# Unread products on TensorE through the head of the run, and two scalar loads moved behind the head of the queues, in a windowed-attention kernel with a gated feed-forward part

## The chip, the cores and the metric

The kernel runs on one core of a Trainium2 chip. The metric is the device time of one execution, in microseconds (us). TensorE is called PE, its weight load PEld, VectorE DVE, ScalarE ACT, GpSimd POOL, SyncE SP.

## What is computed

Two parts, one behind the other; the second takes the output of the first, with the heads side by side, as its x.

```
# q, k, v: 4 batches, 8 heads, 768 positions, 64 wide; n_sink = 4, window = 128
scores = q @ k.T / 8
keep   = (key position < n_sink) or (0 <= query - key < window)
a      = softmax(where(keep, scores, -1e9))          # a / (sum + 1e-9)
x      = a @ v                                        # (4, 768, 512)
h      = relu(x @ w_in);  u, v = halves of h          # w_in (512, 1024)
v_n    = (v - mean) / sqrt(var + 1e-6)                # over 512 columns
v_s    = w_spatial @ v_n + b_spatial                  # w_spatial (768, 768)
out    = (u * v_s) @ w_out                            # w_out (512, 512)
```

w_in and w_out are given in float64; the kernel gets their words and puts the float32 values together itself ("decoding"). n_sink and window are int64 scalars. The kernel has a fast path for 4 and 128 and a general path for anything else; the scalars decide at run time which result stands.

## The kernel before, in words

The work is cut into 48 half tiles: 4 batches, 6 tiles of 128 query positions each, 2 halves of 4 heads. For a half tile PE makes the scores (`sc`), DVE adds the mask and takes the row's smallest value (line 892, `pexp`, `nm`), ACT takes the exponential (line 897), the weights are transposed (in batch 0 by PE, `tr`, line 925, with a copy back to `pT`; later by DMA), PE multiplies them with v (`av`, lines 1005 and 1013), and DVE divides by the sums (`divide`, lines 1020 to 1024, tile `x`). `x` is split into two f16 parts and transposed by DMA (line 1041, `xT`). From `xT` come the v half (`ps_v`, 12 products of 128x512) and, per pair of tiles, the u half (`ps_u`). With a whole batch's v half and w_spatial PE makes `ps_s`, and at the end `ps_o`. Nearly all products are made of three f16 or rounded f32 products (`three`, line 608: high by high, high by low, low by high); in batch 0 the scores and the weights-times-v products are plain f32.

The order of all this is written by a planner in the kernel, class `Plan`. Each piece is added with a rank, its engine, its cost in us, a function that issues it, and the tiles that it reads and writes (`plan.add`). `Plan.order` takes the pieces whose inputs are done, starts the one that can start first in its own account of time (at equal times the one of lower rank), and keeps a ring of buffers per kind of tile. In PSUM there are four banks for `sc` and `tr` together, one double one for `av`, and two for `ps_v`, `ps_u`, `ps_s`, `ps_o` and the one-column products that carry a maximum across partitions (`ps_row`, `ps_col`): that ring is called `mm`. All pieces are then issued in the order of their planned starts, engine by engine, and the engines work their queues off in that order.

The head of the run: SP loads K and q of the first tile, four blocks of w_in's second half, v, and so on (`FIRST_LOADS`). ACT and DVE decode w_in (lines 661 to 671, tile `w`), POOL adds a part (line 674), `all_max` and `scalar` find a scale, and lines 576 and 597 write the two f16 parts (`win`). PE has nothing to do before the first scores.

`read_scalars` (line 35) loads n_sink by SP and window by ACT, each spread over 128 partitions into `words`, as the first DMA of either queue, ahead of the fast path. `tile_kernel` compares them with 4 and 128 after the fast path (lines 1210 to 1216), but the instructions wait only for `words`, and in the built program the conversion (line 41), four comparisons (line 1211), a maximum (line 1213) and a conversion (line 1215) stand at the front of DVE's row. SP reads the flag (line 1216) between two loads of w_in; the other engines read it at the end.

Of the kernel before, what the change touches and what calls it, by code (L numbers as in the profile page):

```python
# [6 lines left out]
F32 = mybir.dt.float32  # L7
# [27 lines left out]
def read_scalars(tc, pool, n_sink, window):  # L35
    nc = tc.nc
    words = pool.tile([P, 4], I32, name="words")
    nc.sync.dma_start(words[:, 0:2], n_sink.bitcast(I32).partition_broadcast(P))
    nc.scalar.dma_start(words[:, 2:4], window.bitcast(I32).partition_broadcast(P))
    wf = pool.tile([P, 4], F32, name="wf")  # L40
    nc.vector.tensor_copy(wf, words)
    return words, wf
# [223 lines left out]
IN_TURN = ("u", "vn", "qkraw", "qp", "pexp", "pT", "p16", "xT", "x16", "av", "sc", "vraw", "vslot0", "vslot1", "vslot2", "vslot3")  # L266
LATENCY = {"PE": 0.25, "d": 0.15, "a": 0.18, "p": 0.12}
# [11 lines left out]
QUEUED = 3.0  # L279
class Plan:  # L280
# [6 lines left out]
    def __init__(self, rings, ring_of):  # L287
        self.pieces, self.rings, self.ring_of = [], rings, ring_of

# [4 lines left out]
    def order(self):  # L294
# [58 lines left out]
        while open_:  # L353
# [46 lines left out]
            for j in after[i]:  # L400
                missing[j] -= 1
                ready[j] = max(ready[j], end)
                if not missing[j]:
                    open_.append(j)
            out.append((t, len(out), f, e))
        if len(out) != n:
            raise RuntimeError("plan: pieces left")
        self.end = max(until.values())
        return [(f, e) for _, _, f, e in sorted(out, key=lambda x: x[:2])]
# [6 lines left out]
def begin(nc, pool):  # L416
# [5 lines left out]
    nc.scalar.activation(first, first, AF.Exp)  # L422
    st.wsp = pool.tile([P, (NT + 1) * S], F32, name="wsp")
# [38 lines left out]
def fast_path(tc, st, qk, v, v0, vs, w_in, w_sp, b_sp, w_out, out):  # L462
# [7 lines left out]
    with (  # L470
# [47 lines left out]
        def next_p16(name):  # L518
# [24 lines left out]
            "ps_o": ("mm", bank("mm")), "ps_row": ("mm", bank("mm")), "ps_col": ("mm", bank("mm")),  # L543
# [617 lines left out]

        W = WHEN
        for t in (0, 2, 4, 5):
            load_v(t)
# [22 lines left out]
        for b in range(B):  # L1187
            gap = W["s gap"]
            for c0 in range(S // TC):
                s0 = 2 * NT * (b + 1) + W["s"] + c0 * (KC * gap + W["s rest"])  # L1190
                for d in range(KC):
                    s_piece(b, c0, d, s0 + d * gap)
                o0 = s0 + KC * gap + W["o"]
                for k in range(TC // P):
                    o_piece(b, c0, k, o0 + k * W["o gap"])
        order = plan.order()
# [5 lines left out]
def tile_kernel(tc, qk, v, v0, vs, n_sink, window, w_in, w_sp, b_sp, w_out, out):  # L1202
    nc = tc.nc
    with tc.tile_pool(name="top", bufs=1) as top:
        with tc.tile_pool(name="first", bufs=1) as pool:
            st = begin(nc, pool)
            words, wf = read_scalars(tc, top, n_sink, window)
            fast_path(tc, st, qk, v, v0, vs, w_in, w_sp, b_sp, w_out, out)
        bad = top.tile([P, 4], F32, name="bad")
        for i, x in enumerate((FAST_N, 0, FAST_W, 0)):  # L1210
            nc.vector.tensor_scalar(bad[:, i:i + 1], wf[:, i:i + 1], float(x), None, op0=ALU.not_equal)
        flag = top.tile([P, 1], F32, name="flag")
        nc.vector.tensor_reduce(out=flag, in_=bad, axis=AX.X, op=ALU.max)
        flagi = top.tile([P, 1], I32, name="flagi")
        nc.vector.tensor_copy(flagi, flag)
        rv = nc.values_load(flagi[0:1, 0:1], min_val=0, max_val=1)
        with tc.If(rv > 0):
            general_path(tc, wf, qk, v, w_in, w_sp, b_sp, w_out, out)
# [45 lines left out]
```

## Time and profile before

| | us |
|---|---|
| median of 3 runs | 443.92 |
| lowest, highest | 441.65, 444.85 |
| span of the profiled execution, first to last instruction | 439.1 |
| what lies around the span, if that execution took the median | 4.8 |
| PE busy | 414.1 |
| DVE busy | 319.1 |
| ACT busy | 272.0 |
| POOL busy | 156.6 |

The profile is of one execution. Times in it count from the span's first instruction. A wait is put down to what ended it last. A stretch is named by its start and end. A transposing load or a scalar load has two times: how long its queue took to issue it, and how long from issue to landing.

### The profile page before, as it was taken

The page shows a single profiled execution, that of the slowest core. Times are in us where ns is not written, and L with a number is a line of the kernel's source. Part 1 is how long each engine was busy: PE and PEld are TensorE (multiplying, and loading weights), DVE is VectorE, ACT ScalarE, POOL GpSimd, SP SyncE. Part 2 cuts the span into 40 slices and gives each one's busy share as a digit, 9 for nine tenths or more (in the row PEclk, how much of TensorE's full clock was granted, in tenths as well). Part 3 has the DMA queues.
Part 4 walks back from the last instruction along what each step waited for, and adds up shares of the span by engine and source line. Part 5 has one row for each costly group of instructions (what it writes and reads, how often), then busy time and mean ns, then how long its engine had stood idle before and what let it go on. Part 6 is the DMA issues. An engine that isn't in the chain of part 4 may idle for free.

```text
span 439.1 us, 9802 instructions
## 1 busy us (share of the span) xinstructions
PE 414.1 (94%) x3669; PEld 323.9 (74%) x3669; DVE 319.1 (73%) x937; ACT 272.0 (62%) x584; POOL 156.6 (36%) x214
## 2 busy tenths in 40 slices
PE   2689999999989999999999999999999999999994
PEld 1467777777677877877778878868778778688882
DVE  3999988689999885878986966788994645143430
ACT  3898978789977565469864754677664353232211
POOL 4426565645735432238351512343541112000000
PEclk9999999999999999999999999999999999999998
DMA  5999414549976784279964673567723822200011
GB/s 215 384 344 296 119 29 115 169 118 196 175 132 162 182 173 133 41 209 208 189 170 123 134 154 87 73 187 154 135 69 98 137 61 64 73 2 24 25 48 57
DMA packets 117928, 59.98 MB, mean 137 GB/s; under 512 B 100240, under 2 KB 103920, under 8 KB 117872
## 3 DMA queue, kind: packets, MB, share of 16 engines
q1 hardware_dynamic: 117728, 59.27, 55.3%
q8 instruction: 31, 0.51, 0.5%
q14 instruction: 25, 0.20, 0.1%
q10 hardware_dynamic: 144, 0.00, 0.0%
HBM read 28.58 MB, written 6.29 MB: 79 GB/s over the span
## 4 chain that ended last, share of the span: by engine, by line
PE 85%; DVE 9%; DMA 2%; issue 1%; ACT 1%; POOL 0%; SPq 0%; ACTq 0%; DVEq 0%
PE ps_s L608 21%; PE ps_o L608 16%; PE ps_v L608 13%; PE ps_u L608 12%; PE sc L887 6%; PE av L1013 4%; PE sc L881 3%; DVE pexp L892 2%; PE tr L925 2%; PE av L997 1%; PE av L999 1%; PE av L998 1%; DMA qkraw<-qk_t 1%; PE av L1005 1%; DVE wsp L597 1%
## 5 line engine op out<-in xcount | busy, mean ns | idle before, releaser
L608 PE MATMUL ps_s<-wsp,vn 128*128 128x256 f16 x864 | 101.0, 273 | 1.6 <-DVE wsp L597 0.8
L608 PEld LDWEIGHTS <-vn 128*128 128x128 f16 x864 | 82.5, 98 | 14.8 <-issue 2.7
L897 ACT ACTIVATE pexp<-pexp,nm 128x260 f32<-128x260 f32 (+1 forms) x192 | 81.2, 484 | 6.2 <-DVE nm L892 6.0
L608 PE MATMUL ps_o<-wout,g 128*128 128x512 f32 x288 | 70.2, 399 | 0.0
L608 PE MATMUL ps_u<-xT,win 128*128 128x256 f16 x576 | 69.0, 273 | 0.4 <-ACT u L1110 0.4
L608 PE MATMUL ps_v<-win,xT 128*128 128x512 f16 x288 | 66.2, 379 | 1.1 <-ACT u L1110 1.1
L608 PEld LDWEIGHTS ps_o<-wout,g 128*128 128x128 f32 x288 | 53.1, 188 | 12.8
L608 PEld LDWEIGHTS <-win 128*128 128x128 f16 x576 | 54.9, 98 | 10.0 <-issue 1.7
L1131 DVE SCALAR_TENSOR_TENSOR g<-ps_s,isc,b_bc 128x256 f32<-128x256 f32 x48 | 23.1, 481 | 39.6 <-PE ps_s L608 38.2
L608 PEld LDWEIGHTS <-xT 128*128 128x128 f16 x288 | 27.0, 98 | 31.5 <-issue 2.2
L574 ACT CAST g<-g 128x256 fp32r<-128x256 f32 x39 | 15.8, 404 | 50.5 <-DVE g L1135 48.3
L590 DVE TENSOR_TENSOR p<-pexp,p 128x1024 f16<-128x1024 f32 (+2 forms) x56 | 40.6, 747 | 8.6 <-ACT p L574 8.6
L590 POOL TENSOR_TENSOR x<-x,x 128x512 f16<-128x512 f32 x24 | 31.2, 1299 | 22.5 <-ACT x L574 21.4
L887 PE MATMUL sc<-kring,qp 64*128 64x260 f32 (+1 forms) x432 | 35.3, 296 | 0.0
L1110 ACT ACTIVATE u<-ps_u,icu 128x256 f32<-128x256 f32 x48 | 22.3, 469 | 17.2 <-PE ps_u L608 17.2
L887 PEld LDWEIGHTS sc<-kring,qp 64*128 64x128 f32 x432 | 28.1, 186 | 6.3 <-issue 4.2
L1078 POOL TENSOR_TENSOR rs<-rs,mhalf 128x1 f32<-128x1 f32 x24 | 16.2, 676 | 46.0 <-DVE rs L1072 42.5
L1157 ACT COPY ob<-ps_o 128x512 f32<-128x512 f32 x24 | 14.1, 586 | 27.9 <-PE ps_o L608 27.9
L574 ACT CAST p<-pexp 128x32 f16<-128x32 f32 (+2 forms) x52 | 30.7, 620 | 0.5
L1068 DVE BATCH_NORM_STATS2 st<-vr 128x6 f32<-128x512 f32 x24 | 16.5, 689 | 17.2 <-ACT vr L1062 17.2
L590 DVE TENSOR_TENSOR g<-g,g 128x256 fp32r<-128x256 f32 x41 | 22.5, 550 | 8.5 <-ACT g L574 7.9
L997 PE MATMUL av<-vring,pT 128*128 128x65 f16 x264 | 27.7, 193 | 0.0
(143 smaller groups left out, 762.5 us busy)
## 6 DMA issues: line engine op xcount, KB each, us to landing
qkraw<-qk_t SPq DMA_DIRECT2D x18, 512.0 KB, 4.4
out<-ob SPq DMA_DIRECT2D x24, 256.0 KB, 2.3
vraw<-v_s SPq DMA_DIRECT2D x18, 256.0 KB, 4.4
dec<-w_in SPq DMA_DIRECT2D x8, 512.0 KB, 6.9
wsp<-w_sp_t SPq DMA_DIRECT2D x6, 384.0 KB, 6.1
dec<-w_out SPq DMA_DIRECT2D x4, 512.0 KB, 4.5
wsp<-qk_t SPq DMA_DIRECT2D x6, 256.0 KB, 5.5
qkraw<-qk_t SPq DMA_DIRECT2D x6, 256.0 KB, 4.4
```

Source lines behind the costliest of these rows:

```text
L574: nc.scalar.copy(o, x)
L590: eng[e].tensor_tensor(out=o, in0=x, in1=hi, op=ALU.subtract)
L608: nc.tensor.matmul(o, a, m, start=(i == 0), stop=(i == n - 1))
L887: nc.tensor.matmul(o, qp[rows, qi, hp, :], keys(kring[:, ki], rows), start=(m == 0), stop=(m == 2))
L897: nc.scalar.activation(po, po, AF.Exp, bias=nm()[:, h2 + q:h2 + q + 1], scale=-1.0)
L997: nc.tensor.matmul(o[:, h], ph, vh, start=(t < 2 and j == 0), stop=False)
L1013: nc.tensor.matmul(o[:, h], pT[:, q * P:(q + 1) * P], v_whole(kt)[:, g:g + D + 1], start=(t < 2 and j == 0), stop=(j == nb - 1 and (t < 2 ...
L1068: nc.vector.bn_stats(s6, vr())
L1078: nc.gpsimd.tensor_tensor(out=vals["rs", i], in0=vals["rs", i], in1=mhalf, op=ALU.pow)
L1110: plan.add(r + WHEN["u relu"], "a", 0.36, lambda e: nc.scalar.activation(tl("u", (b, c0))[:, d, :], tl("ps_u", i)[:, :TC], AF.Relu, scale= ...
L1131: nc.vector.scalar_tensor_tensor(out=g(), in0=tl("ps_s", i)[:, :TC], scalar=vals["s", "sp"][1], in1=b_bc[:, t0:t0 + TC], op0=ALU.mult, op1 ...
L1157: plan.add(r + WHEN["o copy"], "a", 0.5, lambda e: nc.scalar.copy(tl("ob", i), tl("ps_o", i)), [("ps_o", i)], [("ob", i)])
```

## The change

The scalars' loads and comparisons become a class with two steps, `load` and `compare`. Both loads go through SP. The two steps are added to the plan as pieces of rank 27 (`SCALARS_AT`), one on SP, one on DVE; the rank is far behind those of the first tiles (a half tile's rank is its number, from 0 to 47), so that the planner puts them where nothing of lower rank can start.

POOL writes a tile `warm` (128x512, bf16) as its first own work, by an iota. PE gets products of `warm` with itself, 128x128 by 128x256, into a tile of the ring `mm` that nobody reads: 24 as the piece of the lowest rank (-300), and one as a piece of rank 3.2, which reads `x` of the second tile and so waits for its division; the bank is held until then. When the order is made, the planner looks at PE's planned gaps up to that last piece; into each gap of over 0.6 us it puts products for six tenths of the gap less 0.2 us, at 0.11 us each: 82 in twelve gaps, 18 of them between the 24 and the first real product.

```
+    def load(self):
+        for i, x in enumerate(self.sources):
+            self.nc.sync.dma_start(self.words[:, 2 * i:2 * i + 2], x.bitcast(I32).partition_broadcast(P))
+
+    def compare(self):
+        v = self.nc.vector
+        v.tensor_copy(self.wf, self.words)
+        for i, x in enumerate((FAST_N, 0, FAST_W, 0)):
+            v.tensor_scalar(self.bad[:, i:i + 1], self.wf[:, i:i + 1], float(x), None, op0=ALU.not_equal)
+        v.tensor_reduce(out=self.flag, in_=self.bad, axis=AX.X, op=ALU.max)
+        v.tensor_copy(self.flagi, self.flag)
...
+WARM_N, WARM_FIRST = 256, 24
+SCALARS_AT = 27.0
...
         self.end = max(until.values())
+        pe = sorted(x for x in out if x[3] == "PE")
+        last = next(k for k, x in enumerate(pe) if x[1] == self.warm_until)
+        for k in range(last):
+            gap = pe[k + 1][0] - self.ends[pe[k][1]]
+            if gap > 0.6:
+                out.append((self.ends[pe[k][1]], pe[k][1] + 0.5, self.between(0.6 * gap - 0.2), "PE"))
...
+    st.warm = pool.tile([P, 512], BF16, name="warm")
+    nc.gpsimd.iota(st.warm, pattern=[[1, 512]], base=1, channel_multiplier=3, allow_small_or_imprecise_dtypes=True)
...
-            "ps_o": ("mm", bank("mm")), "ps_row": ("mm", bank("mm")), "ps_col": ("mm", bank("mm")),
+            "ps_o": ("mm", bank("mm")), "warm": ("mm", bank("mm")), "ps_row": ("mm", bank("mm")), "ps_col": ("mm", bank("mm")),
...
+        def keep_warm(n):
+            for _ in range(n):
+                nc.tensor.matmul(tl("warm", 0)[:, :WARM_N], st.warm[:, :P], st.warm[:, :WARM_N], start=True, stop=True)
+
         W = WHEN
+        plan.add(-300, "PE", 0.1, lambda e: keep_warm(WARM_FIRST), [], [("warm", 0)])
+        plan.between = lambda t: (lambda e: keep_warm(int(t * 1000 / 110)))
+        plan.add(SCALARS_AT, "SP", 0.8, lambda e: scalars.load(), [], [("words", 0)], dma=0.3)
+        plan.add(SCALARS_AT, "d", 1.3, lambda e: scalars.compare(), [("words", 0)], [("flag", 0)])
...
+        plan.add(3.2, "PE", 0.1, lambda e: keep_warm(1), [("x", (0, 1))], [("warm", 0)])
         order = plan.order()
```

Line numbers of the changed kernel are some 30 higher than those of before for the same work.

PE's row from the start: `sc` are the first tile's scores, `tr` the transposes of the weights, `av` the weights times v, `ps_row` the first of the products that carry a maximum. Before:

```order
L1260 UNCONDITIONAL_BRANCH
L881 MATMUL sc<-wsp,qkraw 128x128 x8
L925 MATMUL tr<-ident,pexp 128x128 x4
L1013 MATMUL av<-vring,pT 128x65 x4
L628 MATMUL ps_row<-ident,allmax_m 1x128
```

After, with the repeated pairs of a weight load and a product left out (42, 4, 13, 5 and 2 of them):

```order
L1291 UNCONDITIONAL_BRANCH
L1193 LDWEIGHTS warm
L1193 MATMUL warm<-warm 128x256
...
L910 MATMUL sc<-wsp,qkraw 128x128 x4
...
L954 MATMUL tr<-ident,pexp 128x128 x4
...
L1042 MATMUL av<-vring,pT 128x65 x4
...
L657 MATMUL ps_row<-ident,allmax_m 1x128
```

42 products now stand ahead of the first score product, and further ones between the pieces of the first tile. The real pieces keep their order up to the first `ps_v`, about 41 us in the trace of before.

The end of that stretch on PE after the change, where the weights of the third tile's first half are turned (`tr`, `sk` its sink columns) and the last unread product stands ahead of the first `ps_v`:

```order
L954 MATMUL tr<-ident,pexp 128x128 x8
L963 MATMUL tr<-ident,sk 16x128
L664 MATMUL ps_col<-allmax_643,ones 128x1
L1193 LDWEIGHTS warm
L1193 MATMUL warm<-warm 128x256
L637 LDWEIGHTS xT
L637 MATMUL ps_v<-win,xT 128x512
```

DVE's row around 50 us of the trace of before: `st`, `mv`, `rs` are the statistics of the first v half, `pT` and `p` copies of transposed weights, `win` the low parts of w_in, `w` blocks of w_out being decoded, `pexp` the masks of the fourth tile's second half. Before:

```order
L1072 TENSOR_SCALAR rs<-mv 128x1
L929 COPY pT<-tr 128x512
L943 COPY p_1_133<-tr 16x128
L597 SCALAR_TENSOR_TENSOR win<-w_356,win_scale,win 128x512
L1086 TENSOR_SCALAR vr<-vr,mv,rs 128x512
L892 ISA pexp,nm<-sc,m_odd 128x260
```

After:

```order
L1101 TENSOR_SCALAR rs<-mv 128x1
L958 COPY pT<-tr 128x512
L626 SCALAR_TENSOR_TENSOR win<-w_470,win_scale,win 128x512
L1115 TENSOR_SCALAR vr<-vr,mv,rs 128x512
L626 SCALAR_TENSOR_TENSOR win<-w_483,win_scale,win 128x512
L52 CAST wf<-words 128x4
L54 TENSOR_SCALAR bad<-wf 128x1 x4
L55 TENSOR_REDUCE flag<-bad 128x1
L56 CAST flagi<-flag 128x1
L688 TENSOR_SCALAR w_805<-w_805 128x512
L688 TENSOR_SCALAR w_824<-w_824 128x512
L921 ISA pexp,nm<-sc,m_odd 128x260
```

Seven instructions that wait for the scalars, and two clamps, now stand ahead of these four masks; two low parts of w_in came forward (the first of the four, and `w_454`'s, stand ahead of the masks of the half tile before).

SP's row behind the second tile's transposing load (`xT`), after the change:

```order
L748 DMA b_bc<-b_sp 128x768
L1070 DMA_TRANSPOSE xT<-x_673 128x8x128
L48 DMA words<-n_sink 128x2
L48 DMA words<-window 128x2
L1247 TENSOR_LOAD flagi
L1247 ISA x2
L631 DMA qkraw<-qk_t 128x512
L1070 DMA_TRANSPOSE xT<-x_896 128x8x128
```

Before, the first of the two scalar loads was SP's first DMA, and the flag was read between the second and third of w_in's later four loads. Now SP reads the flag, which waits for DVE's seven, ahead of the q load and the third tile's transposing load.

## Rows read from the trace of the kernel before

**Rows 1.** The page: PE's busy time (share of the span, instructions) of its first part, and the granted clock in 40 slices, in tenths.

```profile
PE 414.1 (94%) x3669; PEld 323.9 (74%) x3669; DVE 319.1 (73%) x937; ACT 272.0 (62%) x584; POOL 156.6 (36%) x214
...
PEclk9999999999999999999999999999999999999998
```

**Rows 2.** Busy times by stretch: from and to, length, then busy us (and instructions) of each engine, granted clock, share of the DMA engines, GB/s.

```profile
7.40:32.60 25.20, 18.51 (x76) 13.64 (x78) 22.83 (x79) 21.94 (x47) 7.37 (x8) 1.00 1.01 372
...
8.30:36.50 28.20, 21.14 (x98) 15.40 (x96) 26.73 (x90) 24.98 (x53) 9.41 (x9) 1.00 1.01 364
36.50:100.00 63.50, 63.49 (x468) 47.45 (x469) 53.60 (x170) 53.72 (x123) 36.88 (x52) 1.00 0.48 130
100.00:122.50 22.50, 20.72 (x226) 15.67 (x225) 21.29 (x58) 21.81 (x43) 13.71 (x13) 1.00 0.96 185
```

**Rows 3.** The chain of waits in order of time: start, us, what (x is the number of instructions that were put together).

```profile
1.90 5.39 DMA qkraw<-qk_t
...
7.43 0.82 PE sc L881 x4
...
8.35 0.29 DVE pexp L892
...
25.08 2.68 PE sc L881 x7
...
29.66 0.87 PE tr L925 x4
...
36.51 1.49 PE sc L881 x8
...
40.00 0.88 PE tr L925 x8
...
41.29 2.70 PE ps_v L608 x12
...
411.44 5.89 PE ps_s L608 x54
```

**Rows 4.** What DVE waited for between 8 and 37 us (us in total, times, longest).

```profile
DVE pexp L892 <- PE sc L881: 1.8, 1, 1.8
DVE pT L929 <- PE tr L925: 0.8, 1, 0.8
DVE allmax L632 <- PE ps_row L628: 0.2, 1, 0.2
```

**Rows 5.** The transposes on PE by tile, between 10 and 31 us and between 40 and 60: duration in ns, shortest, median, longest; first and last start in us.

```profile
L925 PE MATMUL tr<-ident,pexp x16: 417/418/477, 12.1 to 31.0; 128*128 128x128 f32 x16
...
L925 PE MATMUL tr<-ident,pexp x28: 272/273/281, 39.8 to 59.9; 128*128 128x128 f32 x28
```

**Rows 6.** The start: SP's issues, DVE's and ACT's first instructions behind a load (start, us, instruction, idle time before it); what the DMA engines moved in 40 slices of the first 6 us; and the time from issue to landing of the two scalar loads.

```profile
0.72 0.40 SPq L38 DMA_DIRECT2D words<-n_sink  x1
...
1.18 0.67 SPq L836 DMA_DIRECT2D wsp<-qk_t  x1
...
5.60 0.17 DVE L41 CAST wf<-words 128x4 f32<-128x4 int32 x1 [4.59 <-DMA words<-n_sink]
...
6.36 0.15 DVE L1215 CAST flagi<-flag 128x1 int32<-128x1 f32 x1
...
8.60 0.67 ACT L663 ACTIVATE w<-dec 128x512 f32<-128x512 f32 x1 [5.95 <-DMA dec<-w_in]
...
GB/s 0 0 0 0 0 0 0 0 0 0 0 0 1 1 1 1 1 1 1 1 4 4 8 4 4 4 4 0 11 0 4 7 21 21 157 297 348 348 365 417
...
DMA to landing us min/median/max: 4.6/4.7/4.8
```

**Rows 7.** POOL in order of time: one of its first own instructions, and one of 512 columns later.

```profile
0.86 0.32 POOL L444 MEMSET m_odd<- 128x260 bf16 x1
...
41.44 0.98 POOL L583 TENSOR_SCALAR x<-x 128x512 f16<-128x512 f32 x1 [0.48 <-DVE x L1024]
```

**Rows 8.** PE in order of time, at three of the gaps (idle time before it in brackets).

```profile
12.14 0.87 PE L925 MATMUL tr<-ident,pexp 128*128 128x128 f32 x3 [2.01 <-DVE nm L892]
...
15.20 1.97 PE L1013 MATMUL av<-vring,pT 128*128 128x65 f32 x8 [1.42 <-ACT pT L929]
...
25.08 2.68 PE L881 MATMUL sc<-wsp,qkraw 64*128 64x260 f32 x8 [1.22 <-DMA wsp<-qk_t]
```

**Rows 9.** Around 50 us, in order of time by engine: DVE's division and its rows ahead of the masks, SP's transposing load, PE's transposes; then from the DMA's list of issues (KB each, median us to landing) the slowest load and the transposing loads.

```profile
40.66 0.69 DVE L1024 TENSOR_TENSOR x<-av,den 128x512 f32<-128x512 f32 x1
...
44.58 0.74 DVE L597 SCALAR_TENSOR_TENSOR win<-w,win_scale,win 128x512 f16<-128x512 f32 x1
...
49.57 0.53 DVE L1086 TENSOR_SCALAR vr<-vr,mv,rs 128x512 f32<-128x512 f32 x1
50.02 0.41 DVE L892 CUSTOM_DVE_ANT_0 pexp<-sc,m_odd 128x260 f32<-128x260 f32 x1
...
43.68 1.26 SPq L1041 DMA_TRANSPOSE xT<-x  x1
...
52.39 1.04 PE L925 MATMUL tr<-ident,pexp 128*128 128x128 f32 x8
...
vring<-v_ones SPq DMA_DIRECT2D x2, 520.0 KB, 9.0
...
xT<-x SPq DMA_TRANSPOSE x3, 4.1
```

More of the change, by code (lines that the diff above doesn't have):

```diff
@@ L32, with __init__ @@
 EXP_HIGH = bits_as_f32(0x47F00000)
[L35 to L42, printed above, removed]
+class Scalars:
+    def __init__(self, nc, pool, n_sink, window):
+        self.nc, self.sources = nc, (n_sink, window)
+        self.words = pool.tile([P, 4], I32, name="words")
+        self.wf = pool.tile([P, 4], F32, name="wf")
+        self.bad = pool.tile([P, 4], F32, name="bad")
+        self.flag = pool.tile([P, 1], F32, name="flag")
+        self.flagi = pool.tile([P, 1], I32, name="flagi")
+    def load(self):
[8 more added lines that the diff above has]
+        v.tensor_copy(self.flagi, self.flag)
 def f64_to_f32(nc, raw, w, tmp, top=None):
@@ L288, in __init__ @@
         self.pieces, self.rings, self.ring_of = [], rings, ring_of
+        self.ends = {}
     def add(self, rank, engines, time, f, reads=(), writes=(), dma=None, shared=False):
@@ L404, in order @@
                     open_.append(j)
+            if e == "PE":
+                self.ends[len(out)] = t + d
+                if ("warm", 0) in writes:
+                    self.warm_until = len(out)
             out.append((t, len(out), f, e))
@@ L459, in begin, with fast_path @@
     return st
-def fast_path(tc, st, qk, v, v0, vs, w_in, w_sp, b_sp, w_out, out):
+def fast_path(tc, st, scalars, qk, v, v0, vs, w_in, w_sp, b_sp, w_out, out):
     nc = tc.nc
@@ L1206, in tile_kernel @@
             st = begin(nc, pool)
[L1207 to L1216, printed above, removed]
+            scalars = Scalars(nc, top, n_sink, window)
+            fast_path(tc, st, scalars, qk, v, v0, vs, w_in, w_sp, b_sp, w_out, out)
+        rv = nc.values_load(scalars.flagi[0:1, 0:1], min_val=0, max_val=1)
         with tc.If(rv > 0):
-            general_path(tc, wf, qk, v, w_in, w_sp, b_sp, w_out, out)
+            general_path(tc, scalars.wf, qk, v, w_in, w_sp, b_sp, w_out, out)
 FAST_N, FAST_W = 4, 128
```

## The prediction

> **What bounds the kernel now.** I read the page first: TensorE (PE) is busy for 414.1 of 439.1 us [rows 1]. The busy times by stretch come next, and they split the run: from 36.5 to 100 us PE is busy for 63.49 of 63.50 us, from 100 to 122.5 for 20.72 of 22.50; from 8.3 to 36.5 it is busy for only 21.14 of 28.20, and there VectorE (DVE) has 26.73 of 28.20 [rows 2]. So after 36.5 us every microsecond in which PE waits is a microsecond of the run, and before that DVE sets the pace. The change acts on the head, up to about 55 us, and I judge it by one question: when does PE reach the point at 36.51, from which it runs without a gap?
>
> The chain of waits shows how the head runs: the q load until 7.30, four products, DVE's first mask at 8.35 and its row of work behind it; at 36.51 a score product, and from there PE [rows 3]. In the list of what DVE waited for between 8 and 37 us there is 1.8 us before the first mask, and then only 0.8 and 0.2 us, both for PE [rows 4]. That is the whole share of PE's speed in DVE's pace.
>
> PE's clock. The page's row of the granted clock reads full speed from the start, but the same transpose takes 417 to 418 ns up to 31 us and 272 after 40 [rows 5], and in the chain four take 0.87 us at 29.66 and eight 0.88 us at 40.00 [rows 3]: half speed first, 1.2 GHz against 2.4. The rise fell after 31.0 us and before 40; from 25.08 PE had worked almost without a gap [rows 3, 5, 8]. The granted clock's row shows nothing of the low part.
>
> **The change, part by part.** *Scalars off the front of the queues.* Their load is SP's first instruction, 0.40 us of issue (the K load follows at 1.18), and the bytes moved stay near nothing until 4.8 us although the K load is issued by 1.85; the two small loads landed 4.6 and 4.8 us after issue [rows 6]. Without them the bulk can start between 0.46 us (issue alone) and some 2 us earlier. What it releases is a first product that waited for q (7.43, rows 3) and ACT's first decoding, which waited for w_in (8.60, rows 6). The seven DVE instructions that go with the scalars (5.60 to 6.51, rows 6) ran while DVE had nothing else to do: gain nothing. So this part is worth at most 2 us, and only if nothing else stands in front of PE.
>
> *42 products ahead of the first real one.* The 24, and 18 that the planner puts into its first gap. They stand in PE's queue, so the first real product waits for all of them. One 128x256 product at full clock is 5.89/54 = 0.109 us [rows 3], at half clock 0.218. They can start when POOL has written their operand: the engines begin at 0.72 [rows 6], and the new instruction lies between the nearest rows, 0.32 us (128x260) and 0.98 us (128x512) [rows 7]; I take 0.65, near the middle, and with a hand-over of 0.1 (7.43 + 0.82 to 8.35 at the first mask, rows 3) PE starts at 1.5. All 42 at full clock end at 6.1, all at half at 10.7. The trace of before doesn't say when the clock rises under such a stream; I take half of them at each level, 21 x 0.327 = 6.9 us, so that the first real product starts at 8.4 instead of 7.43. At full clock DVE gets its first mask 0.41 + 0.1 later, at 8.9 instead of 8.35: **+0.55 us**. From there DVE's work up to 36.5 is the same row of instructions in the same order.
>
> *A fast PE in the head.* DVE's two waits for PE, 0.8 and 0.2 us, go [rows 4]: **-1.0 us**. The other 64 products fill gaps: 13 before the first transposes (1.4 us; idle there 2.01), 5 before the first weights-times-v products (0.5; 1.42), 13 before the scores at 25.08 (1.4; 1.22, and the scores before those get 1 us shorter at full clock) [rows 8]. At full clock they fit; at half clock they don't, and then they cost up to what they exceed. I cost them at nothing, since DVE is the later one there. What is late next is DVE itself.
>
> *The last product waits for the second tile's division.* It stands in PE's queue ahead of the first ps_v. The division (x) ends at 40.66 + 0.69 = 41.35; ps_v started at 41.29 [rows 3, 9]. With a hand-over of 0.1 and the product's 0.11 to 0.2, ps_v starts at about 41.6: **+0.3 us**, whole, because PE is the bound from there. Behind it wait all later products.
>
> *The scalars' load and comparison at the new place.* On SP both loads stand behind the second tile's transposing load, and behind them SP waits for the flag; the q load and the third transposing load queue up behind that. On DVE the seven instructions (0.9 us) stand ahead of two clamps and four masks; the planner also moves two w_in low parts ahead of them and the second ps_v ahead of the score product they mask. In the times of before: the transposes are issued until 43.68 + 1.26 = 44.94; words 4.7 us later (49.6) if it takes what it took at the start, 52.5 if it starts when the transposes land (4.1 us, 47.8), at worst 9.0 us like the slowest load (53.9), or one small load after the other, 47.8 + 9.4 = 57.2 [rows 6, 9]. DVE gets there after the normalising at 50.1 and two low parts of 0.74, at 51.6 [rows 9]. PE needs the second of those masks for its next transposes, at 52.39 in before, with ps_v's 2.70 moved ahead at 55.1 [rows 3, 9]; back from it 0.9 + 2 x 0.74 + 2 x 0.41 = 3.2, so DVE may start the scalars as late as 51.9. I take 49.6 to 52.5, nearest the row for this very load: cost 0.
>
> *The new deal of the order from 41 to 122 us.* The same products stand ahead of the first ps_s, in another order. PE's idle time there is 22.50 - 20.72 = 1.78 us in before [rows 2]. It can be less or more; 0, with 1.5 either way.
>
> **Sum**: +0.55 - 1.0 + 0.3 = -0.15 us. The profiled span is 439.1 us; the median of the runs shown, 443.92, lies 4.8 above it, and I add that: 438.95 + 4.8 = **443.8 us**, no change. Bounds of this case: with all 42 at full clock the first mask comes at 6.6 and the sum is -1.75 - 1.0 + 0.3 = -2.45; with the order's 1.5 either way, and two thirds of the products at half clock (first real product at 9.1, +0.7, and some of the 1.0 lost), 440 to 446.5.
>
> **The rivals.** *A: PE's half speed is the head's bound.* PE was busy for 18.51 us between 7.4 and 32.6 [rows 2]; at full clock half of it, 9.3 us, would go: 434.6 us. The page "TensorE: Matmul & The Clock Gate" of the Trainium skill (section "Terms") prices the low clock so: time spent throttled, times the share withheld. By it an estimate for some 31 us at half clock would be 15.5 us, so 428.4. For A speaks that many of PE's early products lie in the chain of waits [rows 3]; against it, that DVE waited for PE for 1 us in all and has 1.5 us of idle time in 28.2 [rows 2, 4]. A rule that counts time at a low clock counts time in which PE wasn't the one waited for.
>
> *B: the scalars' load holds DVE up.* If words lands later than 51.9, DVE stands still, and the masks, the exponentials and PE's transposes behind it with it, one to one. At 57.2 that is 5.3 us: 449.1 us, slower. For it: both loads now stand behind a transposing load on one queue, and either took 4.6 us or more on a queue that was empty [rows 6]. Against it: 49.6 to 52.5 by the nearer rows, and up to 1 us that PE can bridge.
>
> *C: the products don't do what they are for.* If the clock stays low (the real products, with gaps, left it low until 31 us), 42 products end at 10.7, the first mask comes at 10.7 + 0.92 = 11.6 instead of 8.35, DVE's waits stay: +3.25 + 0.3, 447.5 us.
>
> **How the numbers follow.** Forecast 0.72, A 0.09, B 0.11, C 0.08. A measurement of this kernel can tell about 1%, 4.4 us, from no change. Faster by over 1% (below 439.5): A and a thin edge of the forecast's own range, 0.11. Slower by over 1% (above 448.4): B and an edge of C, 0.13. Within: 0.76. The range that leaves out A, and half of B with an edge of C: 440.5 to 448.0.
>
> **What would show it.** Right: in the changed profile PE is busy from about 1.5 us; the first score product starts near 8.4 and takes half as long; the first transposes take 272 ns; DVE has no wait for PE between 10 and 36 us; PE's unbroken stretch begins within 1 us of 36.5; ps_v starts 0.2 us after x. Wrong: an unbroken stretch that begins before 34 (A, or a data start that counts for more than I allow) or after 38 (C); a DVE wait for words of over 1 us followed by a PE wait near 55 us (B); PE idle between 100 and 122 us for over 3.3 us (the order's deal).

## The result, and the profile after

| | before | after |
|---|---|---|
| median of 16 runs each, us | 442.44 | 445.64 |
| lowest, highest | 440.55, 445.54 | 443.33, 450.21 |
| after to before, 95% interval | | 1.0069 (1.0047 to 1.0091) |
| span of the profiled execution, us | 439.1 | 441.5 |
| its own time, us | | 443.33 |

The changed kernel is slower by 3.1 us (0.69%). The forecast was 443.8 us and no change. The ratio leaves out the one execution in the slow state, 450.21 us of after.

The page of after, as in [rows 1] (PE's busy time; the granted clock in 40 slices):

```profile
PE 424.8 (96%) x3776; PEld 331.3 (75%) x3776; DVE 324.0 (73%) x937; ACT 270.1 (61%) x583; POOL 161.0 (36%) x216
...
PEclk9889999989999999999999999999999999999998
```

PE has 107 more products and a span 2.4 us longer. The granted clock has two dips, in the second and third slice and in the ninth; [rows 1] had none before the end.

Busy times by stretch in after (columns as in [rows 2]), with one stretch more:

```profile
7.40:32.60 25.20, 21.33 (x148) 15.60 (x146) 23.44 (x82) 22.70 (x49) 7.94 (x7) 0.86 0.98 349
8.30:36.50 28.20, 24.33 (x171) 18.33 (x170) 27.34 (x95) 25.01 (x53) 10.38 (x9) 0.88 1.01 352
36.50:100.00 63.50, 62.45 (x450) 45.60 (x448) 55.11 (x174) 51.79 (x117) 36.15 (x52) 0.97 0.44 124
100.00:122.50 22.50, 21.45 (x232) 16.26 (x230) 21.69 (x54) 22.02 (x47) 13.74 (x12) 1.00 0.87 172
122.50:150.00 27.50, 24.95 (x238) 19.66 (x236) 26.67 (x68) 17.45 (x37) 14.23 (x13) 1.00 0.70 158
```

The last stretch in before:

```profile
122.50:150.00 27.50, 25.91 (x255) 20.55 (x254) 25.72 (x71) 19.17 (x43) 12.34 (x15) 1.00 0.75 167
```

Read length less PE's busy time. From 36.5 to 100 PE is idle for 1.05 us (0.01 in [rows 2]), from 100 to 122.5 for 1.05 (1.78), from 122.5 to 150 for 2.55 (1.59).

The head and the end on PE in after, in order of time (start, us, instruction, idle time before it in brackets):

```profile
1.44 6.55 PE L1193 MATMUL warm<-warm 128*128 128x256 bf16 x42 [1.44 <-POOL warm L451]
7.92 0.71 PE L910 MATMUL sc<-wsp,qkraw 64*128 64x128 f32 x8
...
12.25 0.77 PE L954 MATMUL tr<-ident,pexp 128*128 128x128 f32 x4 [0.69 <-DVE nm L921]
...
18.80 2.10 PE L910 MATMUL sc<-wsp,qkraw 64*128 64x260 f32 x8
...
26.52 1.15 PE L910 MATMUL sc<-wsp,qkraw 64*128 64x260 f32 x8
...
40.20 0.28 PE L1193 MATMUL warm<-warm 128*128 128x256 bf16 x1
40.54 2.75 PE L637 MATMUL ps_v<-win,xT 128*128 128x512 f16 x12
...
429.53 5.84 PE L637 MATMUL ps_o<-wout,g 128*128 128x512 f32 x24
```

The same end in before:

```profile
426.64 5.84 PE L608 MATMUL ps_o<-wout,g 128*128 128x512 f32 x24
```

Eight score products of one shape take 2.10 us at 18.80 and 1.15 at 26.52: PE was at its lower level between, 1.2 GHz for 2.4 (the records of the granted clock have 18.8 to 25.6). The first `ps_v` comes 0.7 us earlier than in before (40.54; 41.22 in before's row in order of time, 41.29 in the chain of [rows 3]). PE's last product ends at 435.37, in before at 432.48: 2.9 us later. So in these two profiles the head gains 0.7 us, and **the way from the first ps_v to the last product has grown from 391.3 to 394.8 us**. The loss is behind the head.

What DVE waited for between 8 and 37 us in after, as in [rows 4]:

```profile
DVE pexp L921 <- PE sc L910: 7.5, 1, 7.5
DVE allmax L661 <- PE ps_row L657: 0.2, 1, 0.2
```

The 7.5 us lie before the first mask, where DVE now has no scalars to compare.

What PE waited for between 80 and 150 us in after (us in total, times, longest):

```profile
PE ps_s L637 <- DVE wsp L626: 1.4, 1, 1.4
PE ps_u L637 <- ACT u L1139: 1.0, 2, 0.6
PE ps_u L637 <- ACT vr L1091: 0.7, 1, 0.7
PE ps_s L637 <- ACT wsp L605: 0.6, 1, 0.6
PE sc L916 <- DVE nm L921: 0.6, 1, 0.6
```

The longest of these in before:

```profile
PE ps_v L608 <- ACT u L1110: 1.1, 1, 1.1
PE ps_s L608 <- DVE wsp L597: 0.8, 1, 0.8
```

The waits are the same kind, at other places and longer: products that the planner put ahead of the step that frees or fills their tile.

The second dip of the clock, PE in order of time, in after:

```profile
93.76 1.57 PE L916 MATMUL sc<-kring,qp 64*128 64x260 f32 x12
95.27 3.75 PE L637 MATMUL ps_v<-win,xT 128*128 128x512 f16 x12
```

and in before, the same two kinds in a row:

```profile
94.55 1.00 PE L887 MATMUL sc<-kring,qp 64*128 64x260 f32 x12
95.49 2.76 PE L608 MATMUL ps_v<-win,xT 128*128 128x512 f16 x12
```

From the first start to the last end it is 5.26 us against 3.70: 1.56 us lost, in a stretch where PE is the bound. The granted clock was half from 93.9 to 97.3, 3.4 us. The rule of the Trainium skill, page "TensorE: Matmul & The Clock Gate", section "Terms" (throttled time times the share withheld), gives an estimate of 1.7 for it: here the trace agrees. In the head it doesn't: there the full level held for some 20 us longer (5.1 to 40.5 less the 6.8 us of the first dip, against 32.6 to 41.2 in before, by the records of the clock), and the first `ps_v` moved by 0.7 us.

So of the 3.6 us by which the way grew, 1.3 are idle time of PE (4.65 against 3.38 from 36.5 to 150), 1.6 the dip at 94, and 0.7 I can't place.

### The profile page after: what moved, and what is told of

Its sections match the earlier page's. It is cut to its first block, busy times and chain, and to the rows that moved or that the text cites. A ratio compares the mean times of both kernels' runs of the same rounds, so it can differ in the third digit from the quotient of the medians.

```text
span 441.5 us, 10025 instructions
## 1 busy us (share of the span) xinstructions
PE 424.8 (96%) x3776; PEld 331.3 (75%) x3776; DVE 324.0 (73%) x937; ACT 270.1 (61%) x583; POOL 161.0 (36%) x216
## 4 chain that ended last, share of the span: by engine, by line
PE 83%; DVE 10%; issue 3%; POOL 2%; ACT 1%; POOLq 0%; DVEq 0%; ACTq 0%
PE ps_s L637 20%; PE ps_o L637 15%; PE ps_v L637 13%; PE ps_u L637 12%; PE sc L916 6%; PE av L1042 4%; DVE pexp L921 2%; PE sc L910 2%; PE tr L954 2%; PE warm L1193 2%; PE av L1028 2%; PE av L1026 2%; PE av L1027 1%; PE av L1034 1%; DVE w L690 1%
## 5 line engine op out<-in xcount | busy, mean ns | idle before, releaser
L637 PE MATMUL ps_v<-win,xT 128*128 128x512 f16 x288 | 67.2, 383 | 0.1
L619 DVE TENSOR_TENSOR p<-pexp,p 128x1024 f16<-128x1024 f32 (+2 forms) x56 | 41.6, 765 | 6.8 <-ACT p L603 6.8
L619 POOL TENSOR_TENSOR x<-x,x 128x512 f16<-128x512 f32 x24 | 30.0, 1251 | 21.2 <-ACT x L603 20.2
L916 PE MATMUL sc<-kring,qp 64*128 64x260 f32 (+1 forms) x432 | 36.6, 300 | 0.6 <-DVE nm L921 0.6
L619 DVE TENSOR_TENSOR g<-g,g 128x256 fp32r<-128x256 f32 x41 | 23.5, 573 | 8.2 <-ACT g L603 7.6
L1026 PE MATMUL av<-vring,pT 128*128 128x65 f16 x264 | 27.8, 193 | 0.0
L1027 PE MATMUL av<-vring,pT 128*128 128x65 f16 x264 | 27.7, 193 | 0.0
```

The lines of the kernel that those rows point to most:

```text
L619: eng[e].tensor_tensor(out=o, in0=x, in1=hi, op=ALU.subtract)
L637: nc.tensor.matmul(o, a, m, start=(i == 0), stop=(i == n - 1))
L916: nc.tensor.matmul(o, qp[rows, qi, hp, :], keys(kring[:, ki], rows), start=(m == 0), stop=(m == 2))
L1026: nc.tensor.matmul(o[:, h], ph, vh, start=(t < 2 and j == 0), stop=False)
L1027: nc.tensor.matmul(o[:, h], ph, vl, start=False, stop=False)
```

## The experiments

All runs were timed against runs of before on the same chip, those under one heading on one chip. The edits are shortened: "..." stands for what is left out. "Old order" means that PE, DVE and ACT have the sequence of before for everything that before has too. Length: from the start of the first `ps_v` to the end of PE's last product; idle: PE's idle time between 45 and 150 us; both from the one profiled execution, which can lie off its run's median (e10's, 448.00 us, is the longest of its twelve; e3's lies 2.4 above). Clock: mean granted clock, median over the runs (before: 0.996).

| run | order | unread products | scalars' instructions | ratio (95%) | first ps_v | length | idle | clock |
|---|---|---|---|---|---|---|---|---|
| before | old | 0 | front | | 41.22 | 391.3 | 3.37 | 0.996 |
| after | new | 107 | planned | 1.0069 (1.0047–1.0091) | 40.54 | 394.8 | 4.60 | 0.984 |
| e1 | as after | 0 | planned | 1.0040 (1.0027–1.0052) | 40.66 | 394.5 | 5.92 | 0.995 |
| e10 | as after | 0 | late | 1.0062 (1.0035–1.0089) | 43.71 | 395.3 | 6.38 | 0.992 |
| e13 | as after | 107 | late | 1.0054 (1.0031–1.0077) | 40.87 | 395.6 | 3.71 | 0.988 |
| e2 | bank's | 107 | front | 1.0069 (1.0038–1.0101) | 41.66 | 396.9 | 4.72 | 0.984 |
| e6 | bank's | 0 | late | 1.0005 (0.9976–1.0035) | 41.64 | 392.7 | 4.33 | 0.998 |
| e3 | scalars' | 0 | planned | 1.0105 (1.0069–1.0142) | 43.37 | 397.3 | 5.72 | 0.988 |
| e11 | scalars' | 0 | late | 1.0136 (1.0087–1.0185) | 42.98 | 397.1 | 5.74 | 0.985 |
| e14 | old | 0 | planned | 0.9967 (0.9938–0.9996) | 40.18 | 391.5 | 3.69 | 0.998 |
| e4 | old | 0 | late | 0.9985 (0.9960–1.0009) | 41.56 | 391.7 | 3.40 | 0.996 |
| e15 | old | 102 | planned | 1.0027 (1.0001–1.0053) | 41.09 | 393.8 | 4.79 | 0.987 |
| e5 | old | 106 | late | 1.0007 (0.9987–1.0028) | 40.52 | 391.4 | 3.39 | 0.990 |
| e7 | old | 42 ahead | late | 1.0012 (0.9983–1.0042) | 42.28 | 392.0 | 3.40 | 0.972 |
| e8 | old | 64 in gaps | late | 0.9973 (0.9945–1.0002) | 42.51 | 391.6 | 3.42 | 0.987 |
| e12 | old | 18 ahead, 64 in gaps | late | 0.9995 (0.9969–1.0020) | 42.25 | 392.8 | 3.37 | 0.986 |
| e16 | old | 24 in gaps after 20 us | late | 0.9961 (0.9936–0.9986) | 40.13 | 391.7 | 3.65 | 0.997 |

**Order, products or scalars?** e1 keeps the plan of after and issues none of its products:

```
         def keep_warm(n):
-            for _ in range(n): nc.tensor.matmul(...)
+            return
```

> The changed kernel with its planned order, but none of the 107 products is issued (what they would have written is read by nobody). Theory 1, the planner's new order costs the time behind 41 us: the loss stays, ratio to before 1.003 to 1.008, with TensorE idle or at half clock between 80 and 140 us as in the changed kernel. Theory 2, the products themselves cost it (queue ahead of the first scores, clock falls): without them 0.995 to 1.000. Head by either: first scores at 5 to 5.5 us, first mask near 6.5 to 7, first ps_v 0.5 to 2 us earlier than 41.2.

e2 keeps the products as planned and loads the scalars at the front as before:

```
-        plan.add(SCALARS_AT, "SP", 0.8, lambda e: scalars.load(), ...)
-        plan.add(SCALARS_AT, "d", 1.3, lambda e: scalars.compare(), ...)
+            words, wf = read_scalars(tc, top, n_sink, window)
```

> The kernel before with the products as planned pieces (bank held, last one behind the second tile's division), scalars at the front as before. Theory 1 with the products' pieces as what upsets the order: 1.003 to 1.008. Theory 1 with the scalars' pieces as what upsets it: 0.998 to 1.002. Theory 2: 1.003 to 1.010.

e4 has no products and no new piece in the plan; load and comparison are issued when the finished order reaches 150 and 165 us of planned time:

```
+            steps = [(150.0, scalars.load), (165.0, scalars.compare)]
             for f, e, t in order:
+                while steps and t >= steps[0][0]: steps.pop(0)[1]()
```

> The kernel before with its own order; only the two scalar loads and their comparison leave the front and are issued at planned times 150 and 165, outside the planner. No products. Theory 1: the early start of the bulk loads is worth 1 to 2 us and nothing takes it back, ratio 0.995 to 0.998. Theory 2 says the same of this kernel. Rival 3, the scalars' place is what costs: 1.000 to 1.007.

e5 is e4 with the products put in once the order is finished, so that the planner doesn't see them (42 ahead, 64 in gaps):

```
-        plan.add(-300, "PE", 0.1, lambda e: keep_warm(WARM_FIRST), [], [("warm", 0)])
+        plan.begin = lambda e: keep_warm(WARM_FIRST)      # issued ahead of the order
```

> As the kernel with the scalars late and the order of before, plus 106 products: 24 ahead, and six tenths of each planned gap up to the first ps_v; the planner doesn't know of them and no product waits for the second tile's division. Theory 1: the head is as in the changed kernel (first scores at 7.9, first ps_v 40.2 to 40.6), nothing is lost behind it, ratio 0.997 to 1.000. Theory 2: 1.003 to 1.008 as in the changed kernel.

The order alone (e1) is slower than before, with no product issued; with the old order, late scalars (e4) and nearly all products too (e5) can't be told from before. The new order's price is 2.8 us of length (394.5 against 391.7 in e4); the medians of the two, 443.15 and 440.40 us, say the same, and their intervals don't overlap. Most of it is idle time (5.92 against 3.40). What PE waited for in e1 between 80 and 150 us, with no unread product issued:

```profile
PE ps_s L637 <- DVE wsp L626: 1.4, 1, 1.4
PE ps_u L637 <- ACT u L1139: 1.4, 2, 1.0
PE ps_u L637 <- ACT vr L1091: 1.4, 1, 1.4
```

**Which piece upsets the order, which products the clock?** The built orders tell the first: the piece of rank -300 alone and the piece of rank 3.2 alone leave the order of before; both together, which hold one of the two `mm` banks until the second tile's division, give another ("bank's"). The two pieces for the scalars alone give a third ("scalars'"), and the two kinds together that of after. e6 has the bank's order without products, e3 the scalars' pieces alone:

```
e6: +        plan.add(-300, "PE", 0.1, lambda e: None, [], [("warm", 0)])
    +        plan.add(3.2, "PE", 0.1, lambda e: None, [("x", (0, 1))], [("warm", 0)])
e3: -        plan.add(-300, ...)   plan.between = ...   plan.add(3.2, ...)
```

> The two pieces that hold a bank of the ring mm (rank -300, and 3.2 behind the second tile's division) stay in the planner's account but issue no product; the scalars are loaded and compared late, outside the planner's account. The built order of PE, DVE and ACT is that of the run with the products only. Order theory (the held bank makes the planner deal anew, and the new deal costs): first ps_s near 127 us instead of 121.7, PE idle by over 3 us between 41 and 130, 442.5 to 444 us, ratio to before 1.002 to 1.006. Products theory (that run's 1.0069 came from its products and the clock): 440.4 us as with the old order and late scalars, ratio 0.998 to 1.000. Mean granted clock 0.993 to 1.000 by both, since no product is issued.

> The scalars' load and comparison are pieces of rank 27 in the planner's account, as in the change; no unread product, no held bank. Order theory: any new piece re-deals the order, and this deal has its own price: PE's idle time between 80 and 140 us differs from before by up to 1.5 us either way, 439.5 to 443 us. If the held bank alone does the harm: 440 to 441 us, ratio 0.996 to 1.000, as with the scalars late outside the account (440.4). If the scalars' wait does harm (seven DVE instructions ahead of four masks): PE waits for DVE by over 1 us near 55 us and the time is 442 or more. Mean granted clock 0.993 or more.

e7 and e8 are e5 with one half of the products each:

```
e7: -        for k in range(last - 1): ...          # no products in the later gaps
e8: -        plan.begin = lambda e: keep_warm(WARM_FIRST)
    +        plan.begin = lambda e: None            # and none in the first gap
```

> Order of before, scalars late outside the planner's account, the 42 products ahead of the first real one, none in the later gaps. Clock theory A (the block of products ahead is what brings the falls of the clock later): mean granted clock 0.985 to 0.992, 442 us. Clock theory B (the products in the gaps do): mean clock 0.995 or more. The head by both: first real product at 8.4 to 8.7, first ps_v at 40.5 to 41.3 against 41.6 without products, so with B 439.5 to 440.5 us.

> Order of before, scalars late outside the planner's account, the 64 products in the later gaps only, none ahead. The first real product starts at 4.7 us at the low clock. Clock theory A: the clock rises before 32 us and doesn't fall more than in before, mean 0.993 or more, 440 to 441 us. Clock theory B: mean 0.985 to 0.992, 442 us. Products theory without the clock (they cost by their own time in the gaps, at the low clock 0.2 us each): first ps_v after 42 us, 441.5 to 443.

e3 was a miss: 1.0105, the slowest but one of all, with seven small instructions and two loads of 1 KB. The last of its theories had put a time of 442 or more on PE's wait near 55 us, but from 40 to 60 us PE is busy for 20.00 of 20.00 there. e6 is about 1 us longer than e4 and its ratio is open (an interval of 0.6%): it lies between what its two theories had, 1.002 to 1.006 and 0.998 to 1.000. e2 has the same order with the products, and the scalars at the front: 4.2 us longer, with a dip of the clock from 48.0 to 54.8 (6.8 us at half, an estimate of 3.4 lost if nothing hides it), and the intervals of the two don't overlap. On the products neither clock theory holds as written: e7's mean clock fell most, to 0.972, but in its profile all of it, the run's end aside, between 12.4 and 32.9 us, and its head is 0.7 us longer than e4's; e8 was at half from 11.9 to 22.2 and its ratio is the best of these four. The third theory of e8, that the products cost their own time (first `ps_v` after 42), fits its 42.51.

**The scalars' instructions, or only their place in the plan?** e11 is e3, and e10 is e1, with the planned pieces issuing nothing; load, comparison and SP's reading of the flag come late. e13 is after with the same edit. e12 is e5 with `WARM_FIRST` 18 and none in the first gap.

```
-        plan.add(SCALARS_AT, "d", 1.3, lambda e: scalars.compare(), [("words", 0)], [("flag", 0)])
+        plan.add(SCALARS_AT, "d", 1.3, lambda e: None, [("words", 0)], [("flag", 0)])
```

> The pieces for the scalars stay in the planner's account at rank 27, so that every other instruction keeps the order of the run with the scalars' pieces alone (1.0105, ps_v at 43.37), but they issue nothing there; load, comparison and SP's reading of the flag come late, outside the account. If the new deal of the order costs the time: 445 to 447 us, ratio 1.007 to 1.012, first ps_v near 43.4 and PE idle by 4 to 5 us between 122 and 131. If the seven instructions on DVE and SP's wait for the flag cost it: 440.4 to 442 us, ratio 0.998 to 1.000, and that idle time shrinks to below 2.5 us.

> Order of the changed kernel on PE, DVE and ACT, no unread product, the scalars' own instructions late as in the run above. Deal theory: as the run with the order only, 443.2 us, ratio 1.003 to 1.005. Scalars' instructions theory: 440.4 to 441.5, ratio 0.998 to 1.000; first ps_s at 121.5 to 121.9 against 122.34.

> The changed kernel with its 107 unread products in place, only the scalars' own instructions late. Against the run above it prices the products within the changed order. Deal theory with a cost of the products through the clock: 444 to 446 us, ratio 1.004 to 1.008, mean granted clock 0.975 to 0.990. Scalars' instructions theory: 441 to 443 us.

> Order of before, scalars late outside the account, 18 unread products ahead instead of 42 (they end at about 1.4 + 18 x 0.16 to 0.22 = 4.3 to 5.4 us, so that the first real product loses nothing: 4.6 to 5.5), and the 64 in the gaps. If the head can be made shorter by an early start and a fast PE together: first ps_v at 40 to 40.8, 438.5 to 440 us, ratio 0.992 to 0.998. If the head is bound by DVE and the loads whatever PE does: first ps_v at 41 to 42.5, ratio 0.997 to 1.001, as with the gaps only (0.9973).

The instructions cost nothing that these runs can tell: e11, e10 and e13 stay as slow as e3, e1 and after, which have them at their planned place. What PE waited for between 80 and 150 us in e11:

```profile
PE ps_s L630 <- DVE wsp L619: 2.8, 1, 2.8
PE ps_s L630 <- ACT vr L1084: 1.9, 1, 1.9
```

They are the same two waits, to 0.1 us, as in e3: they come from the order. Idle time isn't all of that order's price: in e3 the clock is at half from 95.4 to 98.8 and from 129.5 to 136.4. Within the second fall 18 products of `ps_s` take 4.00 us, and right behind it 2.13:

```profile
131.02 4.00 PE L629 MATMUL ps_s<-wsp,vn 128*128 128x256 f16 x18 [1.90 <-ACT vr L1083]
...
136.36 2.13 PE L629 MATMUL ps_s<-wsp,vn 128*128 128x256 f16 x18
```

e11 has the same two falls within 0.8 us, and the profiles of before, e4 and e14 have neither. e12's shorter head didn't come (first `ps_v` at 42.25).

**Everything in place, the old order back.** The planner counts 1.3 us of DVE for the comparison. With 0.0 instead, the seven instructions stand at the same place of DVE's row as in e3 and everything else returns to the order of before. e14 is e3 with that number; e15 is the whole change with it, and with the bank held to the first tile's division. (In these two, as in e3, the comparison starts at 61.6 to 64.8 us of the trace, in after at 50.69.)

```
-        plan.add(SCALARS_AT, "d", 1.3, lambda e: scalars.compare(), ...)
+        plan.add(SCALARS_AT, "d", 0.0, lambda e: scalars.compare(), ...)
e15 too:
-        plan.add(3.2, "PE", 0.1, lambda e: keep_warm(1), [("x", (0, 1))], [("warm", 0)])
+        plan.add(3.2, "PE", 0.1, lambda e: keep_warm(1), [("x", (0, 0))], [("warm", 0)])
```

> As the run with the scalars' pieces alone (1.0105), but the comparison's piece counts 0.0 us in the planner's account instead of 1.3. The seven instructions stay at the same place of DVE's row, loads and SP's reading of the flag too, and every other instruction of PE, DVE and ACT goes back to the order of before. If the deal alone carries the loss: 440 to 442.5 us, ratio 0.997 to 1.001, length from the first ps_v to PE's last product 391 to 392 us (397.3 in that run). If the scalars' instructions at that place carry some of it: ratio 1.003 or more, and a wait of PE for DVE of over 1 us near 55 us.

> The whole change with two entries of the plan changed: the comparison's piece counts 0.0 us, and the last unread product waits for the first tile's division instead of the second's. PE, DVE and ACT have the order of before, with 102 unread products and the scalars at rank 27 among them. If the deal alone carries the loss: ratio 0.998 to 1.002, 441.5 to 443 us, length from the first ps_v to the last product 391 to 392.5. If the products carry part of it: ratio 1.003 to 1.006, mean granted clock 0.975 to 0.988 with a fall behind 41 us.

e16 is e8 with fewer gaps:

```
-            if gap > 0.6:
+            if gap > 0.6 and self.ends[pe[k][1]] > 20.0:
```

> Order of before, scalars late outside the account, and of the unread products only the 24 in gaps that are planned after 20 us. If the rise of the clock is what moves the head, and a few products bring it before 30 us without a later fall: first ps_v at 40 to 41, mean granted clock 0.995 or more, 438.5 to 440.5 us, ratio 0.992 to 0.997. If the head is bound by loads and DVE in any case, or the clock falls again: ratio 0.997 to 1.001, as with all gap products (0.9973).

e14 against e3 is the cleanest pair: **one number in the plan, the same instructions, and 1.0105 becomes 0.9967**, length 397.3 becomes 391.5. What the planner did with the 1.3 us is seen on DVE, behind the seven instructions. e3, then e14 (`vn` is the normalised v half that `ps_s` reads):

```profile
65.59 0.15 DVE L56 CAST flagi<-flag 128x1 int32<-128x1 f32 x1
66.19 0.43 DVE L913 CUSTOM_DVE_ANT_0 pexp<-sc,m_even 128x260 f32<-128x260 f32 x1 [0.45 <-PE sc L902]
...
62.40 0.15 DVE L56 CAST flagi<-flag 128x1 int32<-128x1 f32 x1
62.47 1.15 DVE L611 TENSOR_TENSOR vn<-vr,vn 128x512 f16<-128x512 f32 x1
63.55 0.42 DVE L913 CUSTOM_DVE_ANT_0 pexp<-sc,m_even 128x260 f32<-128x260 f32 x1
```

With the 1.3 the masks come ahead of `vn`; up to that point the two have one order on PE, DVE, ACT and POOL. So the 3.2 us by which e3's first `ps_v` is later (43.37 against 40.18) aren't the order's: its clock rose at 40.8 us, e14's at 32.6. The length is what shows the deal, and the ratios contain the head too. PE's waits between 80 and 150 us, in e14:

```profile
PE ps_v L629 <- ACT u L1131: 1.2, 1, 1.2
PE ps_s L629 <- DVE wsp L618: 0.8, 1, 0.8
```

e15 says what the deal leaves: at 1.0027 the whole change in the old order is still slower than e14 by 0.6%, so the unread products at their planned places cost too. (The ratio lies between its two ranges, the mean clock fell as the second says, and the fall behind 41 us that goes with it isn't in the profile.) In that profile PE starts the first `ps_v` 0.9 us later than in e14, and a score product waits 1.74 us at 45.6: the profile names nothing that ended the wait, but the product's load of K was issued at 38.28 and took 7.2 us to land, in e14 at 37.50 and 5.1. That the half-clock stretch (14.9 to 21.8) is what made the loads late was not tried. e5 has the products without that wait, and 1.0007.

e16 beats both kernels: 440.19 us against 441.62, and its interval leaves no change out. Against e14 (440.34), which has no product, it is no gain that can be told, so that the earlier rise of the clock (27.8 us) is worth anything isn't shown.

## Why the prediction was wrong, point by point

**The head: right by its terms.** Forecast: PE from 1.5 us, first real product at 8.4, first mask at 8.9. Measured: 1.44, 7.92, 8.56. The 42 products took 6.55 us (6.9). DVE's 0.8 us for PE went and the 0.2 stayed ([rows 4] and above): -0.8 for -1.0. The last unread product took 0.34 us at 40.20 (+0.3). As a sum the head was put at -0.15 and came out at -0.7 in one profile. That the terms make up the 0.7 isn't shown: e1, without any product, has its first `ps_v` at 40.66 for after's 40.54, and the runs without products ahead have it at 40.1 to 43.7.

**Rival A (PE's half speed bounds the head): false**, as a price of the whole head, with the reason given: with PE at full speed for most of the head DVE has 27.34 us of 28.20 there, and `ps_v` moved by 0.7. The rival has a part that I overlooked. Where the clock rose at 27.8 to 34.1 us (before, e1, e4, e6, e14, e16) the first `ps_v` comes at 40.1 to 41.6; where it rose at 40.1 to 41.1 (e3, e10, e11), at 43.0 to 43.7. A rise that late does hold the end of the head up.

**Rival B (the scalars hold DVE up): false.** They landed 3.9 and 3.4 us after issue, from the list of DMA issues of after between 43 and 56 us:

```profile
words<-n_sink SPq DMA_DIRECT2D x1, 1.0 KB, 3.9
words<-window SPq DMA_DIRECT2D x1, 1.0 KB, 3.4
```

DVE reached them at 50.69 without a wait; forecast were 49.6 to 52.5 for the landing and they came at 48.0. e10, e11 and e13 show no cost of the instructions. **Rival C: false** as put; the clock rose at once (transposes at 12.25 at the full level), but it didn't stay.

**The step that failed: "The new deal of the order from 41 to 122 us ... 0, with 1.5 either way".** It measures +2.8 us (e1's length against e4's), +5.4 to +5.8 for the scalars' pieces alone (e11 to e4, e3 to e14). Of e3's 5.8, 2.0 are idle time of PE (5.72 against 3.69); the rest lies where the clock fell at 95 and 129 us. Two things in the step were wrong. The stretch ended at 122, where the first `ps_s` starts, because the same products stand ahead of it; the new waits lie on both sides of that point (in e1 the longest end at 98.7, 103.7 and 126.4), and the sign that I had named (PE idle for over 3.3 us between 100 and 122) stands at 1.05 in after. And the size was taken as if a deal could go either way by chance. Three new orders were run here. Two have a longer way than the old one by far more than its own spread without products (391.3 to 391.7); the bank's, 392.7 in e6, is 1.0 us longer in one profile, and its ratio doesn't tell it from before.

**The clock behind the head: not in the sum at all.** I costed the products in the gaps at nothing and asked only whether the clock rises. It fell again, once where DVE was busy for nearly all of the stretch and once where PE is the bound, for 1.56 us. That such falls are the products' work alone isn't so: e3 and e11 have them with none issued, in the ten executions of e3 the mean clock is 0.985 to 0.991, and e10, which has after's order and no product, has 0.987 to 0.999. The products carry a part that differs from pair to pair: e2 against e6 (where the scalars' place differs too) and e15 against e14 give 0.6%, after against e1 0.3% and e5 against e4 0.2% (intervals that overlap), e13 against e10 nothing. How much of the 3.1 us in after is theirs stays open; the deal's part is shown by pairs without any product, and the two don't simply add.

**The scalars off the front: more than forecast.** "Between 0.46 us (issue alone) and some 2 us" was put for the data's start. What the DMA engines moved in 40 slices of the first 6 us of after:

```profile
GB/s 0 0 0 0 0 0 0 0 0 0 0 0 0 0 17 31 24 116 218 345 352 348 410 403 386 451 355 260 273 273 355 300 273 382 328 382 273 273 273 273
```

It passes 100 GB/s at some 2.6 us, in before at 5.1 ([rows 6]): 2.5 us. Without products ahead the first score product starts at 4.54 to 4.77 for 7.43, 2.7 to 2.9 us earlier. Of the time little follows: 0.3% in e14 (0.04 to 0.6%), and 0.15% in e4, which can't be told from nothing. I take the cause to be that the loads fill the DMA engines from 8 to 36 us ([rows 2], share 1.01), which no run here isolates.

**"+4.8 around the span"**: the executions here whose span and time are both known have 1.8 (after: 443.33 and 441.5). The profiled execution of before took some 440.9 us, below its median; the 3 us that I called overhead were the spread of its runs. I also took 1% for what a measurement can tell from no change; 16 runs each gave an interval of 0.22% either way.

## What to carry to other kernels

When an order is made by a greedy planner, a new entry is a change of the whole order behind it: print the new order, follow it to the end of the stretch where PE is the bound, and charge it, before the entry's own instructions are costed at all. If an instruction needs only a place, give it none of the account (a cost of 0, or insertion after planning) and check that everything else keeps its sequence. No run here shows that fill-in products for the clock pay: 24 of them in late gaps did no worse than none (e16, e14), and 102 cost 0.6% (e15, e14).

## What the runs showed of the hardware that was not expected

The time of the clock's rise differs between runs of one order. e1 and e10 have the same instructions on PE, and in the stretch before 32.6 us their times differ by no more than 0.2 us. PE in order of time, e1:

```profile
30.50 2.10 PE L910 MATMUL sc<-wsp,qkraw 64*128 64x260 f32 x8
32.53 2.26 PE L1042 MATMUL av<-vring,pT 128*128 128x65 f32 x16
34.63 1.04 PE L954 MATMUL tr<-ident,pexp 128*128 128x128 f32 x8
...
40.66 2.76 PE L637 MATMUL ps_v<-win,xT 128*128 128x512 f16 x12
```

e10:

```profile
30.57 2.11 PE L911 MATMUL sc<-wsp,qkraw 64*128 64x260 f32 x8
32.60 3.67 PE L1043 MATMUL av<-vring,pT 128*128 128x65 f32 x16
36.07 1.91 PE L955 MATMUL tr<-ident,pexp 128*128 128x128 f32 x8
...
43.71 1.47 PE L638 MATMUL ps_v<-win,xT 128*128 128x512 f16 x6
```

(The second view ends at 45 us, so its last row has six of the twelve products.) The eight transposes take 1.04 us in one and 1.91 in the other; by the records of the clock the rise came at 33.1 us in e1 and at 41.1 in e10, 8.0 us later, and the first `ps_v` 3.05 us later. That is the head's spread from run to run, as large as what the change moved, and the reason why one profile of either kernel doesn't settle a difference of 0.5%.

The clock also fell without any unread product: in e3 and e11 at 95 us for 3.4 us, in the midst of unbroken work, and at 129 for 6.8, behind PE's wait of 2.8 us. All sixteen executions of these two have a mean clock of 0.985 to 0.991; the twelve of e14 have 0.993 to 1.000. So in this kernel an order of the same work can bring the clock down, by a way that no run here shows.
